# A delta-rule attention with a routed attention behind it: heads on crossed sides, products in 64x64 places, a written order of steps

## The chip, the cores and the metric

One core of a Trainium2 chip (trn2) runs the kernel: TensorE (PE) for matrix products, VectorE (DVE), ScalarE (ACT) and GpSimd (POOL) for the rest, SyncE (SP) issues the DMAs. The metric is the device time of one execution in microseconds, the median of three runs. The profile takes one execution with its span from the first to the last instruction.

## The reference

A first stage per batch and head (4 x 8, 768 tokens, 48 features) is a recurrence over tokens; a second one takes all heads of a token as 384 features and mixes four experts with attention of 64 features, of which the two best by gate count:

```python
for t in range(S):
    kt, vt, bt = (k_n[:, :, t], v[:, :, t], beta[:, :, t, None])
    y[:, :, t] = np.einsum('bhd,bhde->bhe', q[:, :, t], state)
    v_old = np.einsum('bhde,bhd->bhe', state, kt)
    state = state + bt[:, :, :, None] * np.einsum('bhd,bhe->bhde', kt, vt - v_old)
...
for e in range(E):
    q = x @ wq[e]; k = x @ wk[e]; v = x @ wv[e]
    scores = np.where(causal, -1e9, scale * (q @ k.transpose(0, 2, 1)))
    a = softmax(scores)          # row maximum taken off, sum + 1e-9 below
    ye = a @ v @ wo[e]
    out += (e among the two best gates) * w * ye
```

k_n is k over its norm plus 1e-6.

## The kernel before, in words

The work is cut into six units `n`: two batches at a time (n // 3) and a third of the sequence (n % 3), 256 tokens. A unit has four chunks `c` of 64 tokens. In a chunk 16 heads (2 batches x 8) stand as 8 positions `p` with two heads each, one on partitions 0 to 63, one on 64 to 127; 48 of 64 rows hold features, all 64 hold tokens.

Per chunk the kernel forms Gram products of keys with keys and with queries (`gram`; unit 0 also `gram_q`, which multiplies 64 x 64 places), with the keys laid out block-diagonally by ACT copies (`diag_k`). Per unit the recurrence inside the chunks is turned into triangular systems: `st_in` brings 32x32 blocks into a layout in which one partition holds one system, `solve_step` does 31 rank-one steps (unit 0 on DVE and POOL, the others on POOL alone, two instructions per step), `st_nat` and `st_out` bring the blocks back, `merge1` and `merge2` join two blocks of 32 to one of 64. The chain over chunks is then `chain_ks` (state times keys), `chain_u` (solved updates), `chain_q` and `chain_y` (the readout: state part and part inside the chunk), `chain_s` (new state). All these products are fp32; state and updates carry zeros in the other head's half, so a product has 128 rows and 64 columns.

The second stage: `proj_qk` and `proj_v` with split high and low parts (fp32r), 256 columns at a time; `max_list` row maxima of the scores; `score` one expert and two key blocks of 128: a product with 128 rows (high and low keys under each other), one with 64 rows (low queries), one that adds the maxima (bf16), on the diagonal one that adds the mask; `av` values, `norm`, `fin_t`, `fin_o` the output.

The order of instructions on every engine comes from a planner at the end of the function: items with costs, due times and priorities; it takes the best ready item each time and puts `filler` products (zeros, 252 columns) where it reckons that PE would wait or lose its clock. All PE instructions but the transposes go through `mm`, line 38, so PE rows are told apart by tile names: `gp` Gram products of units 1 to 5 and their merges, `px` `chain_ks` (`px<-sb,kq`) and `chain_u` (`px<-xs,tt`), `py` readout, `sp` state, `pm` everything that shares three banks (Gram products of unit 0, projections, scores, output), `po` values (`po<-VS,at`) and fillers (`po<-zb`).

```python
for a, b in ((wqkh, 0), (wqkh, 1), (wqkl, 0)):
    for r in range(3):
        mm(P[:, y], a[:, r, w], xh[:, b, r], j == 0, j == 8)
...
mm(P[:, j, q0:], KA[:, e, b, ks], qa[:, e, b, q0:], True, False)
mm(P[:, j, q0:], KA[h, e, b, ks], ql[h, y, b, q0:], False, False)
mm(P[:, j, q0:], sel[:, e, None].to_broadcast([128, 128]), mr[:, q0:], False, not dg)
```

Of the kernel before, what the change touches and what calls it, by code (L numbers as in the profile page):

```python
# [7 lines left out]
F32 = mybir.dt.float32  # L8
# [19 lines left out]
def tile_kernel(ctx, tc, kq, kv, beta, wqk, wvg, wo, consts, out):  # L28
    nc = tc.nc
    V, S, G, T = nc.vector, nc.scalar, nc.gpsimd, nc.tensor  # L30

    cp = ctx.enter_context(tc.tile_pool(name="cp", bufs=1))
    wk = ctx.enter_context(tc.tile_pool(name="wk", bufs=2))
# [27 lines left out]

    def load_chain(n, c):
        t = wk.tile([128, 2, NP, HD], F32, name="kv", bufs=2)
        nc.sync.dma_start(t, kv[n, c])
        LC[n, c] = t

    def scale_v(n, c):
        vt = LC[n, c][:, 1]
        G.tensor_tensor(vt, vt, PR[n]["nt"][:, c * NP:c * NP + NP, None].to_broadcast([128, NP, HD]),  # L69
                        op=OP.mult)  # L70
        VT[n, c] = vt

    VS = cp.tile([128, 2, 6, NE, EH + 1], F32, name="VS")
    KF = VS.rearrange("p a b c d -> p (a b c d)")
    KT = [KF[:, 384 * c:384 * c + 384] for c in range(CH)]
# [966 lines left out]
```

## Time and profile before

| | us |
|---|---|
| median of 3 runs | 633.92 (631.29 to 635.82) |
| span of the profiled execution | 623.7 |
| between the span and the median | 10.2 |
| busy PE / DVE / ACT / POOL | 586.4 / 337.2 / 302.0 / 279.6 |
| mean granted clock of TensorE | 0.953 |

The profiled execution's own time is its span and what lies around it before the first and after the last instruction; the median of the runs less the span gives the 10.2. An engine is busy from an instruction's start to its end; products on PE are pipelined, so their durations overlap, and the pace is read from start to start.

### The profile page before, as it was taken

The numbers are of one execution on the slowest core, as the hardware profiler recorded it, in microseconds if no ns is written. First come the engines' busy times: TensorE is split into PE (matmuls) and PEld (weight loads), VectorE is DVE, ScalarE is ACT, GpSimd is POOL, SyncE is SP. The second block draws the span as 40 slices with busy tenths as digits, with TensorE's granted clock in tenths as the row PEclk, the third lists the DMA queues.
The fourth block names the chain that finished last, engine by engine and source line by source line (L and its number), as shares of the span: only waits on it lengthen the run. The fifth ranks groups of instructions, "written<-read, shape, count | busy, mean of one in ns | idle before, by whom it ended". The sixth has DMA issues, their size and how long they took to land.

```text
span 623.7 us, 21216 instructions
## 1 busy us (share of the span) xinstructions
PE 586.4 (94%) x9196; PEld 493.0 (79%) x9196; DVE 337.2 (54%) x759; ACT 302.0 (48%) x766; POOL 279.6 (45%) x466
## 2 busy tenths in 40 slices
PE   8797799998999899999989999899999999999997
PEld 6686689877987688897777789788797887977766
DVE  4999723767355817266648306846449333285001
ACT  6652536646574335476336468244462543522333
POOL 6576778820688202889211888103884010000000
PEclk9897889999999959999979999779999999999999
DMA  8500042003410013400102220002101110010001
GB/s 286 213 2 26 27 117 65 2 2 105 121 36 26 2 35 84 115 25 16 39 3 74 71 61 5 26 24 84 53 2 39 42 40 15 14 39 2 1 1 52
DMA packets 16253, 31.10 MB, mean 50 GB/s; under 512 B 2848, under 2 KB 9376, under 8 KB 16160
## 3 DMA queue, kind: packets, MB, share of 16 engines
q1 hardware_dynamic: 16160, 29.75, 15.7%
q8 instruction: 72, 1.18, 0.8%
q14 instruction: 21, 0.17, 0.1%
HBM read 22.66 MB, written 4.72 MB: 44 GB/s over the span
## 4 chain that ended last, share of the span: by engine, by line
PE 67%; DVE 19%; ACT 10%; issue 2%; DMA 1%; POOL 0%; SPq 0%; ACTq 0%; DVEq 0%
PE gp L38 7%; PE po L38 7%; PE px L38 7%; DVE tt L298 4%; PE py L38 3%; PE sp L38 3%; ACT ub L380 2%; DVE mx L532 2%; ACT sb L403 2%; DVE B L201 2%; DVE tn L263 2%; DVE B L261 2%; DVE tn L294 1%; DVE xs L369 1%; DMA VS<-in_kv_dram 1%
## 5 line engine op out<-in xcount | busy, mean ns | idle before, releaser
L261 POOL TENSOR_TENSOR B<-B,tn 128x30 f32<-128x30 f32 (+9 forms) x150 | 78.9, 526 | 11.8
L263 POOL TENSOR_TENSOR tn<-B 128x30 f32<-128x30 f32 (+9 forms) x150 | 73.6, 491 | 10.7
L69 POOL TENSOR_TENSOR kv<-kv,nt 128x384 f32<-128x384 f32 x24 | 20.3, 845 | 110.3 <-DMA kv<-in_kv_dram 66.5
L418 DVE TENSOR_TENSOR xh<-py,xh 112x384 fp32r<-112x384 f32 x24 | 13.4, 557 | 80.5 <-ACT h L417 78.2
L38 PE MATMUL po<-zb 128*128 128x252 bf16 x332 | 50.8, 291 | 1.8 <-DVE zb L43 1.1
L38 PE MATMUL po<-VS,at 128*64 128x65 f32 x1344 | 50.7, 227 | 0.0
L38 PE MATMUL gp<-kq,kd 128*128 128x128 f32 x320 | 46.1, 289 | 4.8 <-ACT pm L169 4.5
L201 DVE STREAM_TRANSPOSE B<-tt 32x1024 f32<-32x1024 f32 (+1 forms) x18 | 35.5, 1970 | 25.0 <-PE gp L38 24.6
L38 PEld LDWEIGHTS po<-VS,at 128*64 128x64 f32 x1344 | 44.4, 139 | 4.2 <-issue 0.5
L38 PEld LDWEIGHTS gp<-kq,kd 128*128 128x128 f32 x320 | 41.0, 198 | 7.9 <-ACT pm L169 7.0
L298 DVE STREAM_TRANSPOSE tt<-B 32x1024 f32<-32x1024 f32 (+1 forms) x18 | 39.4, 2187 | 3.2 <-POOL B L281 3.0
L38 PEld LDWEIGHTS <-zb 128*128 128x128 bf16 x332 | 32.5, 104 | 9.5 <-issue 2.1
L149 ACT ACTIVATE kd<-kq 48x256 f32<-48x256 f32 x86 | 35.6, 415 | 4.2 <-DMA kq<-in_kq_dram 2.4
L380 ACT ACTIVATE ub<-px 64x384 f32<-64x384 f32 x48 | 23.2, 484 | 28.3 <-PE px L38 27.7
L324 POOL MEMSET tt<- 32x512 f32 (+1 forms) x28 | 12.8, 457 | 52.5 <-PE gp L38 47.8
L38 PEld LDWEIGHTS <-sel 128*128 128x128 bf16 x192 | 18.5, 96 | 22.3 <-issue 1.1
L38 PE MATMUL px<-xs,tt 128*64 128x48 f32 x768 | 29.6, 234 | 7.0 <-DVE xs L369 7.0
L190 POOL TENSOR_TENSOR pm<-pm,cst 128x512 f32<-128x512 f32 x24 | 30.2, 1280 | 13.1 <-ACT pm L169 9.9
L38 PEld LDWEIGHTS px<-xs,tt 128*64 128x64 f32 x768 | 26.9, 148 | 9.6 <-issue 6.0
L38 PE MATMUL px<-sb,kq 128*64 128x48 f32 x704 | 29.1, 226 | 3.0 <-ACT sb L403 2.8
L403 ACT ACTIVATE sb<-sp 48x384 f32<-48x384 f32 x44 | 21.3, 484 | 21.1 <-PE sp L38 20.5
L38 PEld LDWEIGHTS px<-sb,kq 128*64 128x64 f32 x704 | 25.2, 140 | 5.6 <-ACT sb L403 5.0
(1732 smaller groups left out, 1499.6 us busy)
## 6 DMA issues: line engine op xcount, KB each, us to landing
kv<-in_kv_dram SPq DMA_DIRECT2D x24, 384.0 KB, 3.8
kq<-in_kq_dram SPq DMA_DIRECT2D x32, 192.0 KB, 3.4
out_dram<-ot SPq DMA_DIRECT2D x24, 192.0 KB, 1.9
xh<-h SPq DMA_DIRECT2D x72, 32.0 KB, 2.0
kq<-in_kq_dram SPq DMA_DIRECT2D x8, 256.0 KB, 5.1
kq<-in_kq_dram SPq DMA_DIRECT2D x4, 512.0 KB, 7.8
VS<-in_kv_dram SPq DMA_DIRECT2D x4, 192.0 KB, 5.4
wst<-in_wqk_dram SPq DMA_DIRECT2D x3, 256.0 KB, 8.0
```

The source lines that it names most:

```text
L38: T.matmul(o, lhsT=a, rhs=b, start=start, stop=stop, skip_group_check=True)
L69: G.tensor_tensor(vt, vt, PR[n]["nt"][:, c * NP:c * NP + NP, None].to_broadcast([128, NP, HD]), op=OP.mult)
L149: S.activation(o, a, AF.Copy)
L190: G.tensor_tensor(pm, pm, pmask[:, None, :].to_broadcast([128, NP, 64]), op=OP.mult)
L201: V.transpose(pr["B"][a], pr["gf"][a, :, o:o + 32].rearrange("p t j -> p j t"))
L261: e.tensor_tensor(X[:, a:b, i + 1:], X[:, a:b, i + 1:], tv, op=OP.add)
L263: e.tensor_tensor(tv, R[:, :, i + 1:].to_broadcast([128, w, m]), X[:, a:b, i:i + 1].to_broadcast([128, w, m]), op=OP.mult)
L298: V.transpose(TG[n % 2][a, :, o:o + 32].rearrange("p t i -> p i t"), PR[n]["B"][a].rearrange("p l i -> p i l"))
L324: G.memset(TG[n % 2][r + 32:r + 64, w * k:w * k + w, 0:32], 0.0)
L380: S.activation(us[r:r + 64, :, h], U[r:r + 64], AF.Copy)
L403: S.activation(st[r:r + HD, :, h], SP[r:r + HD], AF.Copy)
L418: V.tensor_tensor(lo, Y[:, :, 0:3], hi, op=OP.subtract)
```

## The change

Everything but the helpers of the host is written anew; the numbers of the computation stay.

- **Crossed sides.** The head whose features stand on partitions 0 to 63 (`feat(0)`) has its tokens on 64 to 127 (`tok(0)`), the other the reverse. Products of the first stage take 64 (or 48) rows and at most 64 columns: `ga`, `gp` (Gram products, in place of `gram`, without the diagonal copies), `ks`, `tx`, `ku` (in place of `chain_ks`, `chain_u`, `chain_s`). State and updates of a head stand in the two halves of one tile `Z`, keys' masked products and queries in the two halves of `QP`, so the readout `yy` is one product with 128 rows.
- **First solve.** Unit 0 solves two blocks of 16 (`s0`, 14 steps, DVE alone) and joins them by `p1`, `w1`, `p2`, `w2`, `tc0`; then come `m1`, `m2` as before. Units 1 to 5 solve 32 steps on POOL (`sv`); one transpose in (`bi`), two out (`bo`, `tn`); the other blocks are moved by DMAs (`gd`, `to`, `cz`).
- **Projections** `pj`: 512 columns (both halves of the unit at once) but for unit 0, in three parts that the order can place apart; high and low parts in tiles of their own (`KH`, `KL`, `QH`, `QL`), two heads on the two halves.
- **Scores** `sc`: two heads at a time, 64 rows each, four products each (high-high, high-low, low-high, maxima by `SL`), one bank per head; the mask of the diagonal is added by DVE (`sm`). `mx`: high parts, 64 rows; `mr` reduces two banks at once.
- **Order.** `ORDER` is a text of step names (1,696 steps and 15 `fl` entries with 432 fillers of 128 columns); a loop at the end calls each step. `@45` names the PSUM banks.

```diff
+ORDER = """
+zb zz.2 lk.0.2 lk.0.0 lt.0.0 lq.0.0 lc.0 ex0 lk.0.3 lk.0.1 lt.0.1 zz.1 lq.0.3 lk.1.0 lq.1.0 lq.0.1 l3 lt.0.2 lq.0.2
+zz.0 lk.1.2 lc.1 lk.1.1 ww.0 lk.1.3 lc.2 lv.0.0 lv.0.1 lv.0.2 fl.31@2 ga.0.2@1 ga.0.0@2 al.2.1 ae.2.3 ae.2.0 sq.0
...
+tn.0 wl.1 wh.2 bo.0 vs.0.2 ww.3 wl.2 nm.1.1 fl.208@6 p1.0@4 zz.3 ww.4 p1.3@5 nm.1.2 wh.3 wl.3 p1.1@6 w1.0 nm.1.3 wh.4
+p1.2@4 wl.4 ww.5 p2.0@7 w1.1 w1.2 nm.1.4 ww.6 p2.2@4 sv.1.0 wh.5 p2.1@6 wl.5 w2.0.0 w2.2.0 wh.6 w2.0.1 tc0.0.1 w1.3
...
+sv.3.20 sc.1.0.0.1@23 lq.3.3 yh.2.2.0 sv.3.21 av.1.0.0.0@4 yl.2.2.0 sm.1.0.0 sc.1.0.1.1@67 sv.3.22 ex.1.0.0.1 ku.2.2
+sm.1.0.1 sv.3.23 gp.3.3@5 se.2.2.0 lt.3.1 se.2.2.1 sv.3.24 pv.2.0.0@2 pm.3.3.1 yh.2.2.1 ex.1.0.1.1 sv.3.25 yl.2.2.1
...
+def feat(f):
+    return slice(64 * f, 64 * f + HD)
+def tok(f):
+    return slice(64 - 64 * f, 128 - 64 * f)
...
+    def ga(n, c):
+        g, k = slots(("ga", n, c), NP, 64), KF[zi(n, c) % RK]
+        for p in range(NP):
+            for f in range(2):
+                mm(g[tok(f), p], k[feat(f), p], k[feat(f), p])
...
+    def gp(n, c):
+        g, k, q = slots(("gp", n, c), NP, 64), KF[zi(n, c) % RK], QP[zi(n, c) % RQ]
+        for p in range(NP):
+            for f in range(2):
+                mm(g[tok(f), p], k[feat(f), p], q[feat(f), f, p])
...
+    def s0(i):
+        aa = NV[0]["aa"].rearrange("p (x i) -> p x i", x=2)
+        if i < 15:
+            m = 15 - i
+            tv = TM[:, 0:2 * i * m].rearrange("p (x a b) -> p x a b", x=2, a=i)
+            V.tensor_tensor(tv, BX[:, :, i:i + 1, i + 1:].to_broadcast([128, 2, i, m]),
+                            BX[:, :, 0:i, i:i + 1].to_broadcast([128, 2, i, m]), op=OP.mult)
+            V.tensor_tensor(BX[:, :, 0:i, i + 1:], BX[:, :, 0:i, i + 1:], tv, op=OP.add)
+        else:
+            V.tensor_tensor(BX, BX, aa[:, :, :, None].to_broadcast([128, 2, 16, 16]), op=OP.mult)
+            V.tensor_copy(BD(0), NV[0]["aa"])
...
+    def quads(o, a, b, w, t0, qs):
+        for i in range(w):
+            for q in qs:
+                r = slice(32 * q, 32 * q + 32)
+                mm(o[r, i], a(r, t0 + i, 32 * q), b(r, t0 + i, 32 * q))
...
+    def p1(c):
+        g = slots(("p1", c), NP, 32)
+        quads(g, lambda r, t, q: AD[r, t], lambda r, t, q: GF[0][r, t, 32:64], NP, NP * c, (0, 2, 1, 3))
...
+    def w1(c):
+        V.tensor_tensor(W0[:, NP * c:NP * c + NP], slots(("p1", c), NP, 32), W16[:, None, :].to_broadcast([128, NP, 32]),
+                        op=OP.mult)
...
+    def p2(c):
+        g = bank(("p2", c)).rearrange("p (x a b) -> p x a b", x=2, a=NP)
+        quads(g[:, 0], lambda r, t, q: TN[r, t], lambda r, t, q: W0[r, t], NP, NP * c, (1, 3, 0, 2))
+        quads(g[:, 1], lambda r, t, q: W0[r, t], lambda r, t, q: TN[r, t], NP, NP * c, (0, 2))
...
+    def w2(c, q):
+        t = slice(NP * c, NP * c + NP)
+        g = bank(("p2", c)).rearrange("p (x a b) -> p x a b", x=2, a=NP)
+        if q == 0:
+            V.tensor_tensor(GF[0][:, t, 32:64], GF[0][:, t, 32:64], g[:, 0], op=OP.subtract)
+        else:
+            r = slice(64 * q - 64, 64 * q - 32)
+            V.tensor_tensor(TN[r, t], TN[r, t], g[r, 1], op=OP.subtract)
...
+    def gd(n):
+        for r in (0, 64):
+            nc.sync.dma_start(GF[n % 2][r:r + 32, :, 32:64], GF[n % 2][r:r + 32, :, 0:32])
...
+    def to(n):
+        for r in (0, 64):
+            nc.sync.dma_start(GF[n % 2][r:r + 32, :, 0:32], GF[n % 2][r:r + 32, :, 32:64])
...
+    def sv(n, i):
+        aa = NV[n % 2]["aa"]
+        if i == 0:
+            V.scalar_tensor_tensor(B2, B2, -1.0, aa[:, None, :].to_broadcast([128, 32, 32]), op0=OP.mult, op1=OP.mult)
+        elif i <= 30:
+            m = 31 - i
+            tv = TM[:, 0:i * m].rearrange("p (a b) -> p a b", a=i)
+            G.tensor_tensor(tv, B2[:, i:i + 1, i + 1:].to_broadcast([128, i, m]), B2[:, 0:i, i:i + 1].to_broadcast([128, i, m]),
+                            op=OP.mult)
+            G.tensor_tensor(B2[:, 0:i, i + 1:], B2[:, 0:i, i + 1:], tv, op=OP.add)
+        elif i == 31:
+            G.affine_select(B2, B2, pattern=[[-1, 32], [1, 32]], compare_op=OP.is_gt, fill=0.0, base=0, channel_multiplier=0)
+        else:
+            V.tensor_tensor(B2, B2, aa[:, :, None].to_broadcast([128, 32, 32]), op=OP.mult)
+            V.tensor_copy(BD(n), aa)
...
+    def cz(n):
+        for r in (32, 96):
+            nc.sync.dma_start(GF[n % 2][r:r + 32, :, 0:32], Z0[r:r + 32, None, :].to_broadcast([32, NT, 32]))
...
+    def ks(n, c):
+        g, k, z = slots(("ks", n, c), NP, HD), KF[zi(n, c) % RK], Z[zi(n, c) % 2]
+        for p in range(NP):
+            for f in range(2):
+                mm(g[tok(f), p], k[feat(f), p], z[feat(f), f, p])
...
+    def tx(n, c):
+        g, x = slots(("tx", n, c), NP, HD), KV[zi(n, c) % RV][:, 1] if first(n, c) else X
+        for p in range(NP):
+            for f in range(2):
+                mm(g[tok(f), p], GF[n % 2][tok(f), NP * c + p], x[tok(f), p])
...
+    def ku(n, c):
+        g, k, z = P8[:, 0, 0:384].rearrange("p (a b) -> p a b", a=NP), KV[zi(n, c) % RV][:, 0], Z[zi(n, c) % 2]
+        for p in range(NP):
+            for f in range(2):
+                mm(g[feat(f), p], k[tok(f), p], z[tok(f), f, p], first(n, c) and p == 0)
...
+    def yy(n, c):
+        g, q, z = slots(("yy", n, c), NP, 64), QP[zi(n, c) % RQ], Z[zi(n, c) % 2]
+        for p in range(NP):
+            for f in range(2):
+                r = tok(f) if first(n, c) else slice(0, 128)
+                mm(g[feat(f), p], z[r, f, p], q[r, f, p])
...
+    def pj(n, m, h, q):
+        w = 512 if h == 2 else 256
+        g = bank(("pj", n, m, h), w)
+        x, W = XU[n % 2][:, (0, 1, 0)[q]], (WH[0], WH[0], WL[0])[q]
+        for r in range(3):
+            t = x[:, r].rearrange("p h b t -> p (h b t)")
+            mm(g, W[:, r, 128 * m:128 * m + 128], t if h == 2 else t[:, 256 * h:256 * h + 256], q == 0 and r == 0)
...
+    def mx(n, b, i, r):
+        k0, nb, y0, per, sec, g = mv(n, b, i, r)
+        for j in range(per):
+            for x in range(2):
+                e = slice(64 * x, 64 * x + 64)
+                mm(g[:, x, j], QH[e, y0 + j, b, 128 * i:128 * i + 128], KH[e, y0 + j, b, 128 * k0:128 * (k0 + nb)], j == 0)
+        if k0 + nb == 2 * (n % 3) + i + 1:
+            for x in range(2):
+                mm(g[:, x, :, 128 * nb - 128:], IB, MB[:, None, :].to_broadcast([128, per, 128]), False)
...
+    def cells(n, kp):
...
+        if kp < s:
+            return [(2 * kp, 0, 0), (2 * kp + 1, 256, 0)]
+        return [(2 * s + 1, 0, 128), (2 * s, 128, 0)]
...
+    def sc(n, b, y, kp):
+        b0 = BK["sc", n, b, y, kp][0]
+        for j, (kb, o, q0) in enumerate(cells(n, kp)):
+            k = slice(128 * kb, 128 * kb + 128)
+            w = 256 - q0
+            for m in range(4):
+                for x in range(2):
+                    e = slice(64 * x, 64 * x + 64)
+                    a = (KH[e, y, b, k], KH[e, y, b, k], KL[e, y, b, k], SL[e, y])[m]
+                    q = (QH[e, y, b, q0:], QL[e, y, b, q0:], QH[e, y, b, q0:], MR[b][e, q0:])[m]
+                    mm(P8[:, b0 + x, o:o + w], a, q, j == 0 and m == 0)
...
+    def sm(n, b, y):
+        b0 = BK["sc", n, b, y, n % 3][0]
+        g = P8[:, b0:b0 + 2, 0:256].rearrange("p x (j q) -> p x j q", j=2)
+        V.tensor_tensor(g, g, KM[:, None, None, :].to_broadcast([128, 2, 2, 128]), op=OP.add)
...
+    steps = {k: v for k, v in locals().items() if callable(v)}
+    for word in ORDER.split():
+        word, _, at_ = word.partition("@")
+        name, *a = word.split(".")
+        a = tuple(int(x) for x in a)
+        if at_:
+            BK[(name, *(a[:-1] if name in ("pj", "av") else a)) if a else name] = [int(x) for x in at_]
+        steps[name](*a)
 
...
-    def chain_q(n, c):
-        first = n % 3 == 0 and c == 0
-        Y = PY
-        if first:
-            return
-        st, x = SB, LD[n, c]
-        for p in range(NP):
-            for r, h in HA:
-                mm(Y[r:r + HD, p // 4, p % 4], st[:, p, h], x[:, 1, p], p == 0)
...
-    def max_list(n, b, i):
-        s = n % 3
-        nk = 2 * s + i + 1
...
```

## Rows read from the trace of the kernel before

**Rows 1.** The page: busy time by engine; the chain that ended last.

```profile
PE 586.4 (94%) x9196; PEld 493.0 (79%) x9196; DVE 337.2 (54%) x759; ACT 302.0 (48%) x766; POOL 279.6 (45%) x466
...
PE 67%; DVE 19%; ACT 10%; issue 2%; DMA 1%; POOL 0%; SPq 0%; ACTq 0%; DVEq 0%
```

**Rows 2.** Stretches, all work, then fillers: busy us (instructions) by engine, clock, DMA.

```profile
217.70:234.80 17.10, 17.10 (x316) 14.87 (x317) 1.97 (x1) 7.55 (x19) 0.00 (x0) 0.50 0.16 47
...
64.50:623.70 559.20, 532.15 (x8445) 447.72 (x8441) 281.81 (x601) 268.11 (x683) 236.64 (x385) 0.96 0.14 41
...
64.50:623.70 559.20, 22.59 (x135) 11.68 (x135) 0.00 (x0) 0.00 (x0) 0.96 0.14 41
```

**Rows 3.** PE in order of time: start, us, engine, line, tiles, shapes, count.

```profile
237.67 1.09 PE L38 MATMUL px<-xs,tt 128*64 128x48 f32 x32
238.59 1.07 PE L38 MATMUL py<-kq,sb 128*48 128x64 f32 x32
239.49 0.25 PE L38 MATMUL sp<-ub,kv 128*48 128x48 f32 x2
```

**Rows 4.** PE in order of time: a score tile, a merge, values.

```profile
207.51 0.36 PE L38 MATMUL pm__3061<-QA,KA 128*128 128x256 f32 x1
207.80 0.38 PE L38 MATMUL pm__3061<-QL,KA 64*128 64x256 f32 x1
208.11 0.28 PE L38 MATMUL pm__3061<-mr,sel 128*128 128x256 bf16 x1
208.15 0.36 PE L38 MATMUL pm__3071<-QA,KA 128*128 128x256 f32 x1
208.91 0.31 PE L38 MATMUL pm__3071<-QA,KA 128*128 128x128 f32 x1
209.62 1.20 PE L38 MATMUL gp<-tt 32*32 32x32 f32 x64
210.75 1.04 PE L38 MATMUL po<-VS,at 128*64 128x65 f32 x28
```

**Rows 5.** PE in order of time: fillers, 64x64 products of unit 0.

```profile
14.24 0.70 PE L38 MATMUL po<-zb 128*128 128x252 bf16 x5
14.87 1.15 PE L38 MATMUL pm__304<-kq 64*64 64x64 f32 x32
15.95 0.82 PE L38 MATMUL po<-zb 128*128 128x252 bf16 x6
```

**Rows 6.** PE in order of time: a projection, an output product.

```profile
90.92 0.87 PE L38 MATMUL pm__1356<-xh,wqkh 128*128 128x256 f32 x6
...
91.63 0.52 PE L38 MATMUL pm__1356<-xh,wqkl 128*128 128x256 f32 x3
...
406.75 0.51 PE L38 MATMUL pm__5786<-wol,oh 128*128 128x384 f32 x2
...
407.10 0.51 PE L38 MATMUL pm__5786<-woh,ol 128*128 128x384 f32 x2
```

**Rows 7.** DVE and PE in order of time: first solve, first updates.

```profile
24.85 1.29 DVE L248 SCALAR_TENSOR_TENSOR B<-B,aa 128x736 f32<-128x736 f32 x2
...
48.53 0.29 DVE L261 TENSOR_TENSOR B<-B,tn 128x4 f32<-128x4 f32 x2
...
50.53 1.27 DVE L281 COPY B<-aa 128x9 f32<-128x9 f32 x1
...
63.97 1.14 PE L38 MATMUL px<-xs,tt 128*64 128x48 f32 x32
```

**Rows 8.** Groups of instructions: busy us, mean ns of one, idle before.

```profile
L261 POOL TENSOR_TENSOR B<-B,tn 128x30 f32<-128x30 f32 (+9 forms) x150 | 78.9, 526 | 11.8
...
L263 POOL TENSOR_TENSOR tn<-B 128x30 f32<-128x30 f32 (+9 forms) x150 | 73.6, 491 | 10.7
...
L294 DVE STREAM_TRANSPOSE tn<-B 128x1024 f32<-128x1024 f32 x6 | 11.6, 1934 | 0.0
```

**Rows 9.** The page's DMA issues: KB each, median us to landing.

```profile
xh<-h SPq DMA_DIRECT2D x72, 32.0 KB, 2.0
```

More of the change, by code (lines that the diff above doesn't have):

```diff
@@ L62, in load_chain @@
[L62 to L75, printed above, removed]
@@ L208, in square, with sb @@
-    def square(c):
-        if c == 0:
-            solve_vars(0)
-        G.tensor_tensor(SQ[c], KT[c], KT[c], op=OP.mult)
-    def square_sum(c):
-        V.tensor_reduce(PR[0]["ss"][:, NP * c:NP * c + NP], SQ[c].rearrange("p (a b) -> p a b", b=HD), axis=AX.X, op=OP.add)
-    def solve_pre(n, k):
-        pr = PR[n]
-        if n and k == 0:
-            solve_vars(n)
-        ss, g0, r, nn, aa, nt = (pr[x] for x in ("ss", "g0", "rr", "nn", "aa", "nt"))
+    def sb(name, *shape, dt=F32):
+        return cp.tile([128, *shape], dt, name=name)
@@ new lines, in mm, with bank, slots @@
+    def mm(o, a, b, start=True):
+        T.matmul(o, lhsT=a, rhs=b, start=start, stop=True, skip_group_check=True)
+    copy = lambda o, a: S.activation(o, a, AF.Copy)
+    flat = lambda t: t.rearrange("p a b -> p (a b)")
+    P8 = ps.tile([128, 8, 512], F32, name="p8")
+    BK = {}
+    def bank(key, w=512):
+        return P8[:, BK[key][0], 0:w]
+    def slots(key, n, w):
+        return bank(key, n * w).rearrange("p (a b) -> p a b", a=n)
+    KF = [sb(f"kf{i}", NP, 64) for i in range(RK)]
+    QP = [sb(f"qp{i}", 2, NP, 64) for i in range(RQ)]
@@ new lines, in kh, with kl, pv, ve @@
+    def kh(n, m, h):
+        g, a, _ = kqv(n, m, h)
+        copy(a, g)
+    def kl(n, m, h):
+        g, a, b = kqv(n, m, h)
+        V.tensor_tensor(b, g, a, op=OP.subtract)
+    def pv(n, hb, b):
+        g, x = bank(("pv", n, hb, b), 260), XU[n % 2]
+        for q in range(3):
+            for r in range(3):
+                mm(g, x[:, (0, 0, 1)[q], r, hb, b], (WH[1], WL[1], WH[1])[q][:, r], q == 0 and r == 0)
+    def ve(n, hb, b):
+        copy(VS[:, b, 2 * (n % 3) + hb, :, 0:EH], bank(("pv", n, hb, b), 256).rearrange("p (e d) -> p e d", e=NE))
@@ new lines, in mr, with mc, mt @@
+    def mr(n, b, i, r):
+        k0, nb, y0, per, sec, g = mv(n, b, i, r)
+        o = M2[b][:, i] if sec else MP[b][:, i].rearrange("p (x k) -> p x k", x=2)
+        V.tensor_reduce(o[:, :, y0:y0 + per], g, axis=AX.X, op=OP.max, negate=True)
+    def mc(n, b):
+        o = MP[b].rearrange("p i (x k) -> p i x k", x=2)[:, :, :, 0:2]
+        V.tensor_tensor(o, o, M2[b], op=OP.min)
+    def mt(n, b):
+        g = bank(("mt", n, b), 256)
+        for i in range(2):
+            T.transpose(g[:, 128 * i:128 * i + 128], MP[b][:, i], IDN)
@@ new lines, in oh, with ol, fo, oo @@
+    def oh(n, b):
+        copy(OH, bank(("ft", n, b)).rearrange("p (i y q) -> p i y q", i=2, y=2))
+    def ol(n, b):
+        V.tensor_tensor(OL, bank(("ft", n, b)).rearrange("p (i y q) -> p i y q", i=2, y=2), OH, op=OP.subtract)
+    def fo(n, b, i):
+        g = bank(("fo", n, b, i), DM)
+        for q in range(3):
+            for y in range(2):
+                mm(g, (OH, OH, OL)[q][:, i, y], (WH[2], WL[2], WH[2])[q][:, y], q == 0 and y == 0)
+    def oo(n, b, i):
+        copy(OT[i], bank(("fo", n, b, i), DM))
```

1266 lines of the change are left out of this document (439 added, 827 removed).

## The prediction

> **What bounds the kernel now.** I read the page's busy line first, and the shares of the chain that ended last: TensorE (PE) is busy for 586.4 of 623.7 us, VectorE (DVE) for 337, ScalarE (ACT) 302, GpSimd (POOL) 280, and two thirds of the chain are PE [rows 1]. The reader is to see that no other engine is near the span, so a change that moves work from PE to the others can be paid for, and that only PE's own time has to be added up. Then the stretches [rows 2]: from 64.5 us, where the chain over the tokens starts, PE stands still for only 559.2 - 532.15 = 27 us. The granted clock there is 0.96 in the mean; at two levels, 2.4 and 1.2 GHz, this is 8% of the time at half speed, some 22 us lost. Busy is not streaming, though, so the third view is PE in order of time, start to start.
>
> Three prices come out of it, all at the full clock. **Small products:** 32 instructions of a chain step start within 0.92 us (64 weight columns) or 0.90 us (48 columns, 64 moving) [rows 3]. A product of fp32 is two instructions (8 positions x 2 halves x 2 = 32), so a step of 16 products costs 0.93 us; by the same scaling 48 x 48 costs 0.72. A 32x32 step of 64 instructions takes 1.13 us with one change of shape, so 1.02 [rows 4]. **Large products:** a projection product of 256 columns costs 0.71/6 = 0.118 us, an output product of 384 columns 0.35/2 = 0.175 [rows 6]; the line through both gives 0.23 for 512. **Changes of shape:** in a score tile the product with 128 rows is followed 0.29 us later by the one with 64 rows, that one 0.31 us later by the next with 128, while the third gap is 0.04 [rows 4]. Three products of 256 columns at 2.4 GHz are 0.32 us, they take 0.64: the two changes between 128 and 64 rows cost 0.16 each. Changes around 64x64 products are cheaper: 5 fillers (252 columns, 0.105 us) take 0.63, and 32 instructions worth 0.93 take 1.08 [rows 5], so 0.10 into the small shape and 0.15 out of it.
>
> **The change part by part, PE first.**
> Scores. Before, a tile of one head and two key blocks costs 2 x 0.64 = 1.28 us, on the diagonal 208.15 to 209.62, 1.47 [rows 4]; with 16 head-tiles each of 0, 1 and 2 (off) and of 1, 1 and 1 (diagonal) there are 48 of either: 61 + 71 = 132 us. After, two heads go together, rows 0 to 63 for one and 64 to 127 for the other, each into its own bank; 4 products per head and key block, all with 64 rows, so no change of shape inside. If the two row halves overlap, a pair of 256 columns costs 0.12: 24 off-diagonal pairs of heads at 8 x 0.12 and 24 diagonal ones at 0.93 make 45 us. No row here shows two 64-row products that share their columns; the ends are 45 (they overlap as the 64x64 halves do) and 90 (they take turns). I take 45, the nearest row being the 64x64 one [rows 5]. Gain 87.
> Readout. State and new updates stand in the two halves of one tile, so `yy` is one step with 128 rows in place of chain_q and chain_y: 22 steps of 0.90 go, 20 us.
> Gram products. One step of 16 products of 128 columns per chunk becomes two 64x64 steps of 0.93: equal within 1 us. The ScalarE copies that laid keys out diagonally go, off the path.
> Projections. 60 thirds of 3 x 0.23 and 24 of 3 x 0.118 make 50 us against 36 x 12 x 0.12 = 52. Gain 2 to 3. Row maxima: 64 rows and high parts only, 16 us in place of 21 with the masks' share, gain 5 to 7. Values, attention times values, output and merges of unit 1 on: same counts, nothing.
> Fillers. Before has 135 after 64.5 us [rows 2], 14 us at 0.105; after, 170 of 128 columns there, 9 us.
> Changes of shape. Inside the scores they went with the 132 us. Outside I count 181 before (18 us at 0.10) and, going down the written order, 334 from the first `tx` on. About half have a side with 64 rows and 128 columns (0.16), the others 0.10 to 0.15: at 0.13 in the mean 43 us; the ends are 33 (all at 0.10) and 53 (all at 0.16). Loss 25.
>
> In absolute terms, the steps from the first `tx` on stream: 344 us (whole kernel 368, of which 24 lie before it: 13 Gram steps at 0.93 and the merges of the first unit), with fillers 353, with changes 396.
>
> **The start.** Before, the first solve runs from 24.85 to 51.8 us and the first `px<-xs` starts at 63.97 [rows 7]. The 31 steps over 32 columns become 14 steps over two blocks of 16 at once, 28 dependent DVE instructions of at most 112 elements; pairs of tiny ones take 0.3 us, so 28 x 0.3 + 1.5 = 10 us, 17 less. In return come the steps `p1, w1, p2, w2, tc0`, which join the blocks of 16: 10 us of PE (32x32) and 6 of DVE, partly one behind the other, in four parts. I put the first `tx` at 54 us; ends 48 (the joining hidden) and 62 (all in a row).
>
> **What moves to other engines.** The masks of the readout go from POOL to DVE (48 instructions in place of 24), the score masks from PE to DVE (24), ACT loses the diagonal copies and two of three sets of projection copies, DVE four of seven block transposes per unit. Taking these out of the totals of rows 1 and adding the new ones at the duration of their like, I come to DVE 290, ACT 200, POOL 225, against PE's 396 after the start; per unit DVE has 41 to 47 of some 60 us. That is the cover; where DVE fell behind in its order, PE would wait for a `mr` or `pm`. The dropped transposes become DMAs (`to`, `cz`, `gd`): such small copies land after 2.0 us [rows 9]. `cz` stands on the SP queue behind the last `m1`, and `tx` of the next unit waits for it; meanwhile `m2` (1.02 us) and `me` run, so some 1 us per unit shows. The loads queued behind `cz` are wanted several us later, nothing.
>
> **What is late next.** A solve per unit: POOL's 60 instructions take (78.9 + 73.6)/5 = 30.5 us and their gaps 4.5 [rows 8], then the value scaling and norms 7, and on DVE, while POOL stands, two transposes of 1.93 and the square root, some 17 with what lies between: 55 to 60 us per unit. PE has 49 to 54 plus 51 changes, 56 to 61. The two loops are equal within their error, and one queue order couples them; I take 63 per unit. So: first `tx` 54, that of unit 1 near 100, four units of 63 to 352, then the last two stretches of PE (48 and 52 of streaming, 97 changes, 2 of fillers) 116 and waits at the end, 20: 488. The other way, against before: -87 -20 -3 -6 -5 +25 -10 = -106, a span of 518 if all that before loses to waits and the low clock stays; with none of it 54 + 396 = 450. The middle is 484. Around the span lie 633.92 - 623.7 = 10.2 us, which I leave as they are. **Forecast: 500 us**, from the upper of the two.
>
> **A rule that speaks against it.** The 64x64 steps in the kernel before start their 32 instructions in 1.08 us with both halves writing one bank [rows 5]; were the halves to take turns it would be 1.9. The Trainium skill (TensorEngine Tiling (Array Packing), Restrictions and Gotchas) says that different row tiles cannot access the same PSUM bank at the same time; the trace does not bear this out for halves on different partitions.
>
> **The rivals.**
> 1. Waits: the written order leaves PE waiting for the solve loop, at 70 to 73 us per unit, where I have 63, and for DVE at the end. For it: DVE at 70% per unit in strict order; against: 27 us of waiting before. 540 us.
> 2. The 64-row scores and maxima take turns: +45 and +10, 555 us.
> 3. Halves of one bank take turns in every 64x64 step: 94 steps of 0.93 and 22 of 0.72 double, +103: 603 us. Rows 5 speak against it.
> 4. Slower: the clock. For 17.1 us PE was busy without a gap and the clock stood at 0.50 [rows 2]; PE ran mostly 32x32 merges and chain steps then. After the change small products are half of the 353 us of streaming. If the clock stays low for all of them (112 of chain, 39 of attention, 22 of merges), 173 us are added: 673. It is slower than before from 134 us of low-clock streaming on, 38%. Against it: chain steps at 237 us run at the full clock [rows 3], between score tiles.
> 5. Nothing waits and the clock stays: 450 + 10 = 460 us.
> That the change does not do what it says is rival 2 for the scores; elsewhere the diff replaces every stage.
>
> **How the numbers follow.** Forecast 0.60, rival 1 0.16, rival 2 0.10, rival 3 0.02, rival 4 0.06, rival 5 0.06. Range: from 455 (rival 5 with the start at 48) to 560 (rival 2); above lie rivals 3 and 4 and a tail. Faster by over 1%: all but rival 4 and a small remainder, 0.92; same 0.02; slower 0.06. The three runs of before span 0.7%, so 1% is what can be told.
>
> **What would show it.** Score tiles of two heads at 0.96 us start to start; if 1.9, rival 2. `yy` 24 times at 0.90. Changes of shape at 0.10 to 0.19. First `tx` at 54. Granted clock above 0.9; under 0.75, rival 4. Idle PE before `tx` of units 2 to 5 and before `mr`'s readers under 60 us in all; more is rival 1. The prediction is wrong above all if waits in the written order, which no row shows, are far from 50 us.

## The result and the profile after

The kernel after takes 492.0 us (median of 4 runs, 491.0 to 493.1) against 632.7 (631.3 to 635.8): a ratio of 0.779, 95% interval 0.775 to 0.783. The profiled execution took 491.7 us, its span 490.0. The forecast was 500. Here and below, an execution over 1.5% above the fastest of its kernel is left out (one each of the changed kernels of experiments 4 and 9).

The page's busy line and its chain, as in [rows 1]:

```profile
PE 468.3 (96%) x10076; PEld 412.6 (84%) x10076; DVE 282.3 (58%) x561; ACT 196.1 (40%) x393; POOL 217.7 (44%) x416
...
PE 85%; DVE 8%; issue 3%; DMA 2%; ACT 1%; SPq 1%; ACTq 0%
```

The reader is to see that PE has lost 118 us and is still the bound, more than before: 85% of the chain in place of 67. The stretches (all work by engine, granted clock, DMA, as in [rows 2]) are cut at the joining steps, at the first `tx` and at the first `tx` of each unit:

```profile
44.50:63.00 18.50, 12.08 (x588) 11.56 (x589) 12.44 (x30) 5.09 (x13) 6.39 (x16) 0.50 0.09 26
63.00:71.90 8.90, 8.90 (x196) 8.54 (x198) 2.93 (x7) 3.94 (x10) 7.74 (x16) 0.50 0.26 71
...
88.90:92.30 3.40, 3.40 (x23) 3.29 (x20) 0.29 (x1) 0.77 (x2) 2.87 (x7) 0.50 0.09 34
92.30:117.40 25.10, 24.75 (x650) 23.00 (x650) 17.98 (x37) 8.48 (x18) 6.54 (x12) 1.00 0.42 86
117.40:181.40 64.00, 63.30 (x1375) 55.77 (x1375) 41.35 (x88) 26.14 (x56) 41.65 (x84) 1.00 0.32 79
181.40:244.50 63.10, 60.32 (x1321) 52.19 (x1320) 39.15 (x72) 25.69 (x49) 36.51 (x73) 0.95 0.30 76
244.50:305.90 61.40, 61.05 (x1448) 53.05 (x1447) 44.30 (x76) 26.39 (x51) 36.50 (x69) 1.00 0.33 85
305.90:368.30 62.40, 62.40 (x1358) 54.35 (x1357) 31.80 (x65) 27.11 (x56) 36.59 (x67) 1.00 0.22 56
368.30:490.00 121.70, 118.47 (x1825) 100.18 (x1823) 51.64 (x102) 52.13 (x94) 11.03 (x23) 1.00 0.10 31
```

From 117 us on PE hardly stands still and the clock is full but for a dip in unit 2. The first two rows are the other kind: 18.5 us in which PE is busy for 12, then 9 us busy throughout, both at 0.50.

PE in order of time, two score tiles of two heads, one behind the other; they answer to [rows 4]:

```profile
466.75 0.39 PE L183 MATMUL p<-qh,kh 64*128 64x256 f32 x2
466.97 0.28 PE L183 MATMUL p<-ql,kh 64*128 64x256 f32 x2
467.09 0.28 PE L183 MATMUL p<-qh,kl 64*128 64x256 f32 x2
467.21 0.28 PE L183 MATMUL p<-mr,sl 64*128 64x256 f32 x2
...
467.79 0.28 PE L183 MATMUL p<-qh,kh 64*128 64x256 f32 x2
...
468.62 0.28 PE L183 MATMUL p<-mr,sl 64*128 64x256 f32 x2
468.83 0.92 PE L183 MATMUL p<-vs,at 128*64 128x65 f32 x24
```

A pair, one product of 256 columns for each head, starts 0.12 us after the one before: eight pairs are the 0.96 us of the forecast. The first pair, behind a change of shape, holds 0.22 us, so the first tile takes 1.04. From the last pair of the second to the values 0.21 us pass: 0.09 of them are the change of shape.

PE in order of time from the first solve's end to the chain, to be held against [rows 7]:

```profile
42.29 1.75 PE L183 MATMUL p<-gf,at 32*32 32x32 f32 x182 [2.29 <-DVE gf L412]
46.01 1.22 PE L183 MATMUL p<-gf,at 32*32 32x32 f32 x73 [1.97 <-issue]
...
49.74 0.36 PE L183 MATMUL p<-at,tn 32*32 32x32 f32 x9 [1.71 <-issue]
...
53.40 0.37 PE L183 MATMUL p<-tn,at 32*32 32x32 f32 x6 [1.00 <-issue]
...
57.13 1.23 PE L183 MATMUL p<-gf 32*32 32x32 f32 x39 [1.09 <-issue]
...
60.59 0.47 PE L183 MATMUL p<-tn,at 32*32 32x32 f32 x10 [0.77 <-issue]
...
62.97 1.95 PE L183 MATMUL p<-kv,gf 64*64 64x48 f32 x32 [0.33 <-ACT gf L498]
64.84 1.06 PE L183 MATMUL p<-gf 32*32 32x32 f32 x32
```

The joining (`p1, p2, m1, m2`) takes 20.7 us and has five gaps, 6.5 us in all, "issue" each: PE waited for nothing that the profile shows. They come every 3.5 to 3.7 us, and between one gap and the next PE starts 128 matmuls (one lot has 127 in the trace; the rows in between are left out here). The first `tx` starts at 63.0, where before the first `px<-xs` started at 63.97.

The forecast's account beside the trace:

| stretch | forecast | measured |
|---|---|---|
| up to the first `tx` | 54 | 63.0 |
| unit 0 | 46 | 54.4 |
| units 1 to 4 | 252 | 250.9 |
| last two stretches | 136 | 121.7 |
| span | 488 | 490.0 |
| around the span | 10.2 | 1.7 |

Units 1 to 4 agree; the four other parts are off by 8 to 14 us each, with both signs.

### The profile page after: what moved, and what is told of

It reads as the page before. It is cut to its first block, busy times and chain, and to the rows that moved or that the text cites. A ratio compares the mean times of both kernels' runs of the same rounds, so it can differ in the third digit from the quotient of the medians.

```text
span 490.0 us, 22373 instructions
## 1 busy us (share of the span) xinstructions
PE 468.3 (96%) x10076; PEld 412.6 (84%) x10076; DVE 282.3 (58%) x561; ACT 196.1 (40%) x393; POOL 217.7 (44%) x416
## 4 chain that ended last, share of the span: by engine, by line
PE 85%; DVE 8%; issue 3%; DMA 2%; ACT 1%; SPq 1%; ACTq 0%
PE p L183 82%; PE p L749 1%; DVE tm L404 1%; DVE vs L406 1%; DMA kf<-in_kq_dram 1%; PE p L675 1%; DVE tn L415 1%; DMA xu<-h 1%; SPq L575 1%; DVE b L471 1%; DVE qp L334 1%; DVE at L342 1%; DVE gf L412 0%; DMA qp<-in_kq_dram 0%; DVE ss L363 0%
## 5 line engine op out<-in xcount | busy, mean ns | idle before, releaser
L465 POOL TENSOR_TENSOR tm<-b 128x30 f32<-128x30 f32 (+9 forms) x150 | 72.8, 485 | 34.5 <-DVE rs L736 14.3
L467 POOL TENSOR_TENSOR b<-b,tm 128x30 f32<-128x30 f32 (+9 forms) x150 | 77.7, 518 | 11.8
L711 ACT ACTIVATE at<-p 128x768 f32<-128x768 f32 (+1 forms) x48 | 43.4, 916 | 34.7 <-PE p L183 21.5
L185 ACT ACTIVATE z<-p 48x384 f32<-48x384 f32 (+1 forms) x68 | 33.0, 486 | 45.5 <-PE p L183 40.7
L666 DVE TENSOR_REDUCE mp<-p 128x2 f32<-128x1024 f32 (+3 forms) x40 | 44.2, 1115 | 11.1 <-PE p L183 10.6
L183 PE MATMUL p<-vs,at 128*64 128x65 f32 x1344 | 47.2, 224 | 0.6 <-issue 0.6
L183 PEld LDWEIGHTS p<-vs,at 128*64 128x64 f32 x1344 | 42.3, 137 | 6.4 <-issue 3.4
L183 PE MATMUL p<-xu,wh 128*128 128x512 f32 (+1 forms) x168 | 43.6, 399 | 0.3 <-DMA xu<-h 0.3
L334 DVE TENSOR_TENSOR qp<-p,cs 64x512 f32<-64x512 f32 x48 | 32.9, 688 | 8.6 <-PE p L183 7.9
L183 PE MATMUL p<-kf 48*64 48x64 f32 x768 | 31.6, 243 | 2.5 <-DMA kf<-in_kq_dram 2.5
L533 DVE COPY z<-p 64x384 f32<-64x384 f32 x24 | 13.5, 561 | 26.5 <-ACT z L185 21.4
```

The source lines that it names most:

```text
L183: T.matmul(o, lhsT=a, rhs=b, start=start, stop=True, skip_group_check=True)
L185: copy = lambda o, a: S.activation(o, a, AF.Copy)
L334: V.tensor_tensor(QP[zi(n, c) % RQ][r, f], slots(("gp", n, c), NP, 64)[r], PMK[r, None, :].to_broadcast([64, NP, 64]), op=OP.mult)
L465: G.tensor_tensor(tv, B2[:, i:i + 1, i + 1:].to_broadcast([128, i, m]), B2[:, 0:i, i:i + 1].to_broadcast([128, i, m]), op=OP.mult)
L467: G.tensor_tensor(B2[:, 0:i, i + 1:], B2[:, 0:i, i + 1:], tv, op=OP.add)
L533: V.tensor_copy(o, a)
```

## The experiments

Each kernel is the one after with one edit; its time stands beside 492.0, its ratio against the kernel before beside 0.779. The kernel before was run again beside each set of them (medians of 628.8 to 632.0 us), so where time and ratio differ by a few tenths of a per cent, the ratio counts.

**1. The halves in turn.** In `sc` the loop over the two heads moves outside the loop over the four products:

```diff
-            for m in range(4):
-                for x in range(2):
+            for x in range(2):
+                for m in range(4):
```

> In every score tile the four products of one head now come before the four of the other, so the two 64-row halves of the array stand in a row instead of side by side. If the gain of the scores comes from the overlap (a pair of 256 columns in 0.12 us, 48 tiles of two heads in 45 us), each product costs 0.12 by itself: 24 tiles off the diagonal get 0.96 us longer and 24 on it some 0.74 to 0.93, together 41 to 45 us, and the kernel takes 533 to 537 us. If the halves take turns already, or if the scores lie beside a wait, it stays at 492 to 496 us.

Measured: 493.2 us, 0.780 (0.774 to 0.785), no change. But not because the halves take turns. PE in order of time in this kernel:

```profile
463.01 0.28 PE L183 MATMUL p<-qh,kl 64*128 64x256 f32 x1
463.01 0.28 PE L183 MATMUL p<-ql,kh 64*128 64x256 f32 x1
463.13 0.27 PE L183 MATMUL p<-mr,sl 64*128 64x256 f32 x1
463.13 0.28 PE L183 MATMUL p<-qh,kl 64*128 64x256 f32 x1
463.24 0.28 PE L183 MATMUL p<-qh,kh 64*128 64x256 f32 x1
463.25 0.28 PE L183 MATMUL p<-mr,sl 64*128 64x256 f32 x1
```

Two products still start together every 0.12 us, but they are different ones: one head's `qh,kl` beside the other's `ql,kh`, and at 463.24 the first product of one head's next key block beside the last of the other's present one. The order that was written has slipped: as far as the names tell, a product starts beside one that was written up to three places away. The experiment hadn't taken the overlap away, so it says nothing of its worth; the next one does.

**2. One row half for both heads.**

```diff
-                    e = slice(64 * x, 64 * x + 64)
+                    e = slice(0, 64)
```

> Both heads of a score tile are computed from rows 0 to 63 of keys, queries, maxima and selection, so the odd heads get the scores of the even ones and their output is wrong; number, shape, places in PSUM and order of the products are those of the kernel after. When the order within a tile was changed (four of one head, then four of the other) the time stayed and the trace shows products of the two row halves starting in the same moment still. If it is the two row halves running side by side that makes a pair of 256 columns cost 0.12 us, this takes that away whatever the order: 24 tiles at 0.96 us more and 24 at 0.74 to 0.93 more, 41 to 45 us, 533 to 537 us, and pairs in the last stretch start 0.23 us apart. If a product of 64 rows costs 0.06 by itself, it stays at 491 to 494 us.

Measured: 537.9 us (536.2 to 541.9), 0.857 (0.848 to 0.865): 45.8 us more. PE in order of time:

```profile
508.04 0.40 PE L183 MATMUL p<-qh,kl 64*128 64x256 f32 x2
508.27 0.40 PE L183 MATMUL p<-mr,sl 64*128 64x256 f32 x2
508.51 0.40 PE L183 MATMUL p<-qh,kh 64*128 64x256 f32 x2
```

The pairs start 0.235 us apart. So the overlap is what halves the scores, and it is worth what the forecast took between its ends of 45 and 90. The row maxima `mx` weren't changed here; in the kernel after their two halves start together too, 3 to 4 ns apart.

**3. The readout twice.** `yy` issues its products a second time into the same place.

```diff
+        for _ in range(2):
             for p in range(NP):
                 for f in range(2):
```

> Each readout step of 128 rows is issued twice into the same place (the second writes the same values). Before the change a chunk had two steps there, and the forecast priced the one that went at 0.90 us, 20 us in all. Theory A, TensorE's own time sets the end in every unit: 24 more steps of 0.90 us, 510 to 514 us. Theory B, in units 1 to 4 the loop through the solve on GpSimd and VectorE sets the 63 us per unit and TensorE has room: only the 4 steps of the last unit and the 4 of the first show, 496 to 500 us.

Measured: 508.9 us, 0.803 (0.798 to 0.809), 16.8 more. In the profiled runs units 1, 3 and 4 and the last stretch get 3.1, 3.6, 3.6 and 3.6 us longer, close to 4 x 0.90; units 0 and 2 don't (+0.5 and -0.6). Theory A where the step shows; the price of 0.90 holds.

**4. Scores without the low parts.** `for m in (0, 3)` in place of `range(4)`.

> The two products of every score with a low part (high by low, low by high) are left out, so the scores are less precise; nothing else is changed. TensorE has about half of its 45 us of scores less. Theory A (TensorE's own time sets the end everywhere): 20 to 23 us less, 469 to 472 us. Theory B (the loop through the solve sets the 63 us per unit): only the 20 of 48 tiles that come after the last chain start at 368 us show, 8 to 10 us less, 482 to 484 us.

Measured: 475.0 us (470.8 to 475.8), 0.748 (0.741 to 0.754), 17.0 less: between the two, nearer A. The last stretch gives back 7.9, unit 4 3.7, unit 3 2.9, unit 2 only 0.2, at a clock of 0.92 there.

**5. Half of each solve.**

```diff
         elif i <= 30:
+            if i % 2:
+                return
```

> Of the 30 dependent steps of each solve of units 1 to 5 on GpSimd only every second is done, so the inverses are wrong; 30 of 60 GpSimd instructions per unit go, about 15 us of its 30 us in each solve. Theory A (TensorE's own time sets the end): 488 to 493 us, the unit period stays at 61 to 64 us. Theory B (the loop through the solve): the period of units 1 to 4 falls from 63 towards TensorE's own 56 to 58, and the kernel takes 465 to 475 us.

Measured: 491.8 us (486.1 to 493.1), 0.774 (0.768 to 0.781): no change. The stretches of units 2 and 4 in this kernel, and of unit 2 in the second kernel of experiment 9, whose solves are untouched:

```profile
179.85:238.72 58.87, 57.33 (x1320) 49.55 (x1319) 38.57 (x72) 25.68 (x49) 20.26 (x38) 1.00 0.31 82
```

```profile
299.98:362.37 62.39, 62.39 (x1356) 54.35 (x1355) 31.84 (x65) 27.11 (x56) 21.10 (x38) 1.00 0.22 56
```

```profile
182.18:240.88 58.70, 57.28 (x1319) 49.65 (x1318) 38.80 (x72) 25.68 (x49) 37.32 (x73) 1.00 0.32 82
```

GpSimd (the fifth figure of a row) has lost 15 of its 36 us, and unit 4 takes 62.4 as before. Unit 2 seems to gain 4 us here; but it takes 58.7 with a full solve too. What it loses in the kernel after is mostly the clock, 0.95 in its row above against 1.00 in both of these. The solve sets the end in none of the units 1 to 5.

**6. Projections in halves.** Each 512-column product as two of 256 (180 become 360).

> Each projection product of 512 columns is issued as two of 256 columns with the same weights, as before the change: 180 products become 360. By the line through 256 and 384 columns a wide one costs 0.23 us and two halves 0.236, so 1 us in all: 492 to 494 us. If the wide form saves a fixed price per product (0.02 to 0.03 us, a weight load that does not hide), 3 to 6 us: 495 to 498 us.

Measured: 492.3 us, 0.782 (0.777 to 0.788). The wide form is worth nothing that can be told.

**7. No fillers.** Every `fl` leaves the written order.

> All fillers, products of zeros that nothing reads, are left out: 262 before the first tx and 170 behind it. If the granted clock does not need them, the 170 give back their price, 9 us, and changes of shape with them: 480 to 485 us. If the clock falls for lack of them in the stretches where they stand, the steps there run at up to twice their time and the kernel takes 492 to 515 us.

Measured: 491.5 us (487.0 to 492.3), 0.779 (0.771 to 0.787): neither. From the first `tx` to the end the span has 425.1 us against 427.0, not the 9 less of their price, and unit 0 runs at a mean clock of 0.82 in place of 0.89.

**8. Four stretches behind the end,** which measure the gaps and the changes of shape by themselves. `tiny(m)` is m times four products of 32x32, `half()` 16 products of 64x48, `wide(m)` m products of 512 columns:

```python
wide(40)
if k == 0:
    tiny(128)
elif k == 1:
    for _ in range(16):
        tiny(8)
        wide(5)
elif k == 2:
    for _ in range(16):
        half()
    wide(16)
else:
    for _ in range(16):
        half()
        wide(1)
```

> Four stretches of products that nothing reads are added behind the last output product, each after 40 products of zeros with 512 columns, so that the clock is up; all four are longer than the kernel by what they take. First, 512 products of 32x32 in a row (1024 matmuls): 15 to 17 us by their price of 1.0 us for 64; 26 to 31 us if every 256 instructions wait for a 16 KB block that needs 3.5 to 3.9 us (theory C). Second, the same 512 in groups of 32 with five products of 512 columns after each: the wide ones add 17 us and 31 changes of shape; by theory C the gaps of the first are gone and it takes 36 to 39 us in all; without it 33 to 37, no less than the first plus 20. Third, 16 steps of 16 products of 64x64 in a row and then 16 products of 512 columns: 18 to 19 us. Fourth, the same with one wide product after each step: 31 changes of shape more; at 0.10 to 0.16 us each, 3 to 5 us longer than the third; if changes of shape cost nothing, the same as the third.

PE in order of time, the beginnings of the first, second and fourth stretch:

```profile
490.22 1.60 PE L183 MATMUL p<-cs 32*32 32x32 f32 x167
494.09 1.27 PE L183 MATMUL p<-cs 32*32 32x32 f32 x128 [2.27 <-issue]
497.84 1.93 PE L183 MATMUL p<-cs 32*32 32x32 f32 x128 [2.47 <-issue]
501.86 1.93 PE L183 MATMUL p<-cs 32*32 32x32 f32 x128 [2.09 <-issue]
...
528.34 0.75 PE L183 MATMUL p<-cs 32*32 32x32 f32 x64
529.02 1.25 PE L183 MATMUL p<-zb 128*128 128x512 bf16 x5
530.20 0.75 PE L183 MATMUL p<-cs 32*32 32x32 f32 x64
...
592.41 0.92 PE L183 MATMUL p<-cs 64*48 64x48 f32 x32
593.26 0.39 PE L183 MATMUL p<-zb 128*128 128x512 bf16 x1
593.58 0.92 PE L183 MATMUL p<-cs 64*48 64x48 f32 x32
```

First stretch: after the first 167 matmuls PE gets exactly 128 at a time, every 3.75 to 4.02 us, and waits 1.8 to 2.5 us before each lot, at either clock. 128 matmuls with their weight loads are 256 instructions; in these 28.5 us (26 to 31 expected by theory C) the queue for instruction code moved 8 blocks, 0.13 MB. The DMA view of that stretch (packets, MB, share of 16 engines):

```profile
q8 instruction: 8, 0.13, 2.2%
```

Second stretch: the same 512 products and 80 wide ones take 31.0 us, 2.5 more than the tiny ones alone, and from 528.34 to 551.49 no gap is left. The size was off (36 to 39 expected), since 64 tiny matmuls with the change of shape behind them need 0.69 us here and not 1.0; the gaps are the code's. In a row, a wide product takes 0.216 us. At that price the third stretch takes 15.6 us and the fourth 18.7: 30 more changes of shape cost 3.1 us, 0.10 each, the lower end of what was expected.

**9. Wide fillers in the joining,** two products of 512 columns, then one, behind each of 12 of its steps:

```diff
-p1.0@4 zz.3 ww.4 p1.3@5 nm.1.2
+p1.0@4 fw.2 zz.3 ww.4 p1.3@5 fw.2 nm.1.2
```

> Behind each of 12 steps of the joining before the first tx (p1, p2, m1, m2 of unit 0), two more products of zeros with 512 columns are issued: 24 of them, 5.2 us at the full clock and 10.3 at half. Theory C: in that stretch TensorE waits for its instructions (gaps of 2.0, 1.7, 1.0, 1.1 and 0.8 us, 6.6 in all, each ending with a 16 KB block of instruction code). The fillers need 48 instructions, next to nothing to load, so they lie in those gaps: the first tx starts within 1.5 us of 63.0, the granted clock of the stretch from 44.5 to 72 us rises, and the steps behind it run in about half their time: 486 to 491 us. Theory D, the gaps are something else that each step brings with it (a wait that the profile does not show): the fillers are added to it, the first tx starts at 68 to 73, and the kernel takes 494 to 500 us.

> One product of zeros with 512 columns behind each of the 12 joining steps, in place of the two of the run before: 12 of them, some 0.24 us each at the full clock, 0.45 at half as two fillers took there, 2.9 to 5.4 us in all, less than the 6.6 us of gaps. Theory C (the gaps are the loading of instruction code, one 16 KB block in 3.4 to 4 us): the time from p1 to the first tx stays at 20.7 us within 1.5, and the gaps shrink by what the fillers take. Theory D (the gaps are waits of the steps themselves): 23.5 to 26 us. The whole kernel 490 to 495 us by C, 494 to 499 by D.

Measured: with two, 492.7 us (487.9 to 494.3), 0.781 (0.773 to 0.789), the first `tx` at 69.7, 26.5 us behind `p1`; with one, 488.4 (487.7 to 490.4), 0.776 (0.771 to 0.782), the first `tx` at 66.7, 23.5 behind `p1`. Theory C's times are missed both times, and theory D's time for the first `tx` is met both times, once at its edge. What the gaps do is C's all the same: D would have left them standing, and they went, from 9.8 us of "issue" waits over the whole kernel to 2.5 and 3.3. But with 24 wide products too the clock, 1.00 from 50 to 56 us, stood at 0.50 to 0.52 from there to the first `tx`; a filler costs 0.45 us at that level, and from the seventh step on (56 us) no gap is left for the fillers to lie in. So the fillers cost more than the gaps they fill. Where gaps were left, the clock was not the reason. PE in order of time with one wide product a step, its clock at 1.00 from 47 to 53 us:

```profile
50.83 0.32 PE L183 MATMUL p<-at,tn 32*32 32x32 f32 x14 [1.52 <-issue]
...
54.66 0.64 PE L183 MATMUL p<-tn,at 32*32 32x32 f32 x16 [1.74 <-issue]
```

The two gaps end 3.83 us apart, as in the first stretch of experiment 8, with 127 matmuls between them. The 3.6 us by which the second kernel is below 492.0 come with a full clock in unit 2 (58.7 us), which the fillers at 45 to 66 us do not explain; the intervals overlap, and no gain is claimed.

**10. The first solve over 32 columns again,** without `p1, w1, p2, w2`; then, in a second kernel, with the weight splits placed ahead of the clearing of the tile that the solve uses.

```diff
-        if i < 15:
-            m = 15 - i
-            tv = TM[:, 0:2 * i * m].rearrange("p (x a b) -> p x a b", x=2, a=i)
...
+        if i < 31:
+            m = 31 - i
+            tv = TM[:, 0:i * m].rearrange("p (a b) -> p a b", a=i)
```

> The first solve is put back to 32 columns: 30 dependent steps on VectorE in place of 14 over two blocks of 16, and the joining steps p1, w1, p2 and w2 are left out (one product of zeros gives PSUM bank 7 its first values); m1, m2 and all else stay. Theory E, the joining gives back what the shorter solve gained (10 us of chain gained, p1 and p2 some 12 us of TensorE with gaps for instruction code lost): first tx at 61 to 65 us, where the kernel after has 63.0. The forecast's arithmetic, the new start is worth 10 us: first tx at 71 to 74. In either case the norms and the solve of unit 1 start later by the 17 us that VectorE is busy longer, so unit 1 may wait for its solve: 490 to 508 us by theory E, 500 to 515 by the other.

> As the run with the first solve over 32 columns, and the weight splits that stood behind the clearing of the tile in which the solve works (GpSimd, and through it the loads and ScalarE's copies) now stand ahead of it, so that ScalarE is free when the first merge wants it; there TensorE waited 7.1 us for it, and the first tx was at 69.4 us. Theory E (the shorter solve gained no more than the joining steps cost): first tx at 61 to 64 us, the kernel 485 to 491 us, 1 to 6 less than the run before it in the median, and not slower than the kernel after. The forecast's arithmetic (the shorter solve is worth 10 us of start): 71 to 74 us for the first tx and 497 to 503 us.

Measured: 494.8 us (490.4 to 496.7), 0.785 (0.778 to 0.792), and 494.3 (491.9 to 497.7), 0.786 (0.781 to 0.790); the first `tx` at 69.4 and 68.8. Both theories miss it. PE in order of time, first kernel, then second:

```profile
58.28 1.92 PE L182 MATMUL p<-gf 32*32 32x32 f32 x64 [21.59 <-DVE gf L414]
67.31 0.90 PE L182 MATMUL p<-at,tn 32*32 32x32 f32 x26 [7.11 <-ACT at L184]
...
69.38 0.88 PE L182 MATMUL p<-kv,gf 64*64 64x48 f32 x12 [0.33 <-POOL gf L504]
```

```profile
63.98 1.06 PE L182 MATMUL p<-at,tn 32*32 32x32 f32 x32 [1.33 <-ACT at L184]
67.44 0.79 PE L182 MATMUL p<-gf 32*32 32x32 f32 x21 [2.39 <-DVE qp L337]
```

Once ScalarE is free, the next wait is VectorE's, whose norms of unit 1 and readout masks stand behind the longer solve. As written, the shorter solve with its joining is worth 3 to 6 us at the first `tx` (63.0 to 65.7 in the kernels that have it and no wide fillers) and 2 to 3 in the medians, whose intervals overlap with that of the kernel after; what a written order made for the long solve would give wasn't tried.

## Why the prediction was right, and where its account was not

**Scores, right.** 0.12 us a pair, 0.96 a tile; experiment 2 gives the other end, 45.8 us more. Rival 2 is out. **Readout, right:** 0.90 a step (experiment 3).

**64x64 steps, right.** PE in order of time, at the full clock:

```profile
97.64 1.10 PE L183 MATMUL p<-kf 48*64 48x64 f32 x32
98.67 1.10 PE L183 MATMUL p<-qp,z 128*48 128x64 f32 x32
99.70 1.57 PE L183 MATMUL p<-xu,wl 128*128 128x256 f32 x11
```

A Gram step of two halves in one bank takes 1.03 us with the change of shape behind it, 0.90 to 0.93 without. The same trace, instruction by instruction, has its 32 starts in 16 pairs, 7 ns apart, one pair every 58 ns: the halves start together, and turns at that price would make the step 1.9. Rival 3 is out. The Trainium skill (TensorEngine Tiling (Array Packing), Restrictions and Gotchas) says that different row tiles cannot access one PSUM bank at the same time. No cost of that kind shows here for halves on different partitions; whether their writes fall in one moment, starts can't tell.

**Changes of shape, number and price about right.** After the first `tx` the trace has 333, forecast 334. With two halves that start together counted as one step, the last step before a change holds PE 0.09 us longer than the same step elsewhere (mean of 273 at the full clock), out of every form alike: 0.09 to 0.10. The first step behind a change holds it another 0.05 in the mean, most for 64x128 and 128x128 (0.07 and 0.06), least for 32x32 (0.02). Where only the tiles change and not the shape, both are 0.00 in the median. That makes 0.15 a change and some 49 us, forecast 0.13 and 43, its ends 33 and 53; experiment 8 has 0.10 for one pair of shapes. The split by form that the forecast made (0.16 where 64x128 is on one side, 0.10 to 0.15 elsewhere) hardly shows in these figures. **Projections, right:** a small gain forecast, none that can be told (experiment 6).

**Fillers, a term mis-sized:** 5 us of gain were counted from having fewer; taking all away gives nothing that can be told (experiment 7), so their 9 us stand largely where PE would wait or run at the low clock.

**Units, right in size, wrong in reason.** 63 us was taken above two loops held to be equal, the solve at 55 to 60 and PE at 56 to 61. Experiments 3 to 5 show PE alone: unit 4 has 62.40 us busy of 62.40, and halving the solve leaves it at 62.4; only unit 2 can't tell, since its clock differs from run to run. PE's own time was put a little low; rival 1 is out.

**Other engines, right:** DVE 282, ACT 196 and POOL 218 busy for 290, 200 and 225, and no wait of PE for `cz`.

**The start, the step that failed.** The solve runs from 23.2 to 35.7 us, 12.4 for "28 x 0.3 + 1.5 = 10 us", and ends within 1 us of where the forecast had it. What failed is the joining: 10 us of PE and 6 of DVE "partly one behind the other", with a first `tx` at 54 and an outer end of 62. It took 20.7 us from `p1` on. 6.5 of this are the gaps, which no row of before suggested in that size: there the small products stand between large ones. Experiment 8 shows what such gaps are, one block of code for 256 instructions every 3.75 to 4 us. The joining gets the same lots of 128 matmuls with their 128 weight loads, one every 3.5 to 3.7 us, so from 46 us on the code sets its pace. The clock stood at 0.50 from 44.5 to 71.9 us as well, but a full clock alone would not have made the joining shorter as far as the other traces show: the lots came 3.75 and 3.83 us apart at the full clock too (experiments 8 and 9).

**Unit 0, mis-sized by the same clock:** 54.4 for 46. A chain step there takes 1.87 us at 0.50 (62.97 to 64.84) for 0.93; 8.9 us run like this, and another 3.4, a projection, from 88.9 to 92.3, which accounts for some 6 of the 8. The rest is a wait of 2.5 us for a load of keys (`kf`), ended at 88.0. Rival 4 was right only that far: from 92.3 us on the small products run at the full clock but for the dip in unit 2, and the kernel is nowhere near the 134 us of low clock that it needs. Rival 5 fell with the same two terms, the start and the low clock.

**The tail, mis-sized the other way:** 116 of PE and 20 of waits forecast, 121.7 in all. PE is busy for 118.5; some 3 us of waits, not 20.

**Around the span, a wrong reading.** 10.2 us were the median of the runs less the span of another execution. After, the same subtraction gives 2 us, and the profiled execution has 1.7 around its span. The kernel before has no more: of its executions beside the experiments one took 631.84 us with a span of 630.1. So some 8.5 of the 10.2 us were the difference between two executions, added to a kernel that doesn't have them.

So the total came out within 2% because +9 and +8 at the start met -14 at the tail and -8 around the span. That these four nearly cancel is luck. The prices of scores, readout and 64x64 steps held; the serial parts were estimated without such prices.

## What to carry to other kernels

Two 64-row halves of TensorE ran side by side in both orders in which their products were written; what decided was which rows a product uses, and that was worth a factor of two. When a step is split into many small products, count its instructions as well as its columns: beyond 256 in some 4 us the code did not come fast enough here. Fewer instructions help then, or wide work between them that has to be done anyway; products of zeros cost more than the gaps they filled. A chain that is cut in half must be priced with what joins the halves. And the span of a profile is taken from the time of the same execution, not from the median of others.

## What the runs showed of the hardware that was not expected

- 64 matmuls of 32x32, with the change of shape behind them, take 0.69 us (10.8 ns each) at the full clock while their code lasts; in a row they run at 30 ns each (128 in 3.75 to 4.02 us) once it has to be loaded, at either clock (experiment 8).
- The Trainium skill (Runtime: NRT & Kernel Launch, Instruction fetch mechanics) says that an engine's code is refilled in blocks of 16 KiB, 256 instructions, while the current ones run, and that crossing a block's end is mostly hidden. The blocks agree with experiment 8; "hidden" holds there only where wide products stand between the small ones, and in a row of small ones 1.8 to 2.5 us of each 3.75 to 4.02 are waits.
- The two row halves don't keep to the order written: a product starts beside one that was written three places earlier or later (experiment 1).
- The clock stood at 0.50 between 44.5 and 71.9 us in the kernel after while PE was busy two thirds of the time to 63.0 us and all of it from there; 24 wide products among the small ones went with a full clock from 50 to 56 us and a low one from there on (experiment 9). What would raise it there stays open.
- Over the kernels here whose edit leaves unit 2 alone, its granted clock is 0.95 to 1.00 and its time 63.1 to 57.6 us; two kernels that differ by 5 us in one profile need not differ.
